# Two key-weight loads moved from SyncE's queue to ScalarE's at the start of a fused attention and GeGLU kernel

## The chip, the core and the metric

The kernel runs on one core of one Trainium2 chip. The time is the device time of that core in microseconds (us), from one launch to its end. Lower is better. Profiles are of one execution, taken by the hardware profiler.

## What is computed

The input x has 2048 rows of 640 values in bf16. The result mixes two blocks by a gate that each row computes for itself:

```python
g = sigmoid((x * gate_w).sum(-1))
qkv = x @ wqkv                      # 640 x 1920, 32 heads of 20
pq, pk = phi(q), phi(k)             # phi(t) = t + 1 where t > 0, else exp(t); plus 1e-6
kv = einsum("bhsd,bhse->bhde", pk, v); z = pk summed over the rows
a = (pq @ kv) / (pq . z + 1e-6) @ wo
b = (gelu(x @ w_gate) * (x @ w_up)) @ w_down     # 640 x 1728, 1728 x 640
out = g * a + (1 - g) * b
```

## The kernel before

The rows are taken in 16 tiles of 128. Every matmul contracts over 128 partitions, so the 640 input features make five chunks, numbered 0 to 4, and a product of a row tile with a 640-wide weight is five steps. A step needs the transposed tile (features on the partitions, `xT`) as the stationary operand and one chunk of 128 weight rows as the moving one.

All instructions are recorded in program order by a small planner (`P.op`), one list for each engine. It works out from the buffers read and written which semaphores an instruction waits for; it reorders nothing. So the order in the source is the order on each engine, and the order of the DMAs on each of the two queues that issue them, SyncE's (SP) and ScalarE's (ACT).

The order of work on TensorE (PE) is:

1. The first stage, which the change is in. A few matmuls on constants (`warm`), then the transposes of row tile 0 on TensorE (`T`, L439, copied out by VectorE in L443), then the key products of row tiles 0 to 3, and then their query products. `KM(n, [k])` is one step, chunk k, of the key product of row tile n: one matmul over 512 columns (L459) and one over 128 (L460), into two PSUM banks of the tile's own. `QM` (L474, L475) is the same for queries, with one extra column, the gate. `gate_col` (L504, L506) turns the gate weights into that column. After each of these products `phi1` (ScalarE, L484 and L488) and `phi2` (VectorE, L494 and L498) apply phi.
2. Key and query products of row tiles 4 to 15 (`KQ`, L545).
3. The sums over rows (`MM`, L602, L605, L612, L617), the feed-forward's first two products (`G`, L706), the small attention matrices (`KV`, `W2`), and the output products (L827 to L880).

The first stage's inputs come from DRAM. `load_x` (L349) brings a row tile as it is; `load_wk` (L352) brings one chunk of the key weights, 128 rows of 1280 bytes, 160 KB; `load_wq` (L360) one chunk of the query weights; all three end in `dma_in`, whose one line the profile calls L343. `load_xT` (L355) is a transposing DMA that writes row tile i straight into `xT`. Row tile 0 alone is transposed by TensorE. `gw_sb` holds the gate weights. The loads are put into the two queues like this (the first of ScalarE's is a load of 128 bytes, L368):

```python
load_x(0)
load_wk(0)
load_xT(1)
load_wk(3)
load_wk(4)
load_wk(1, "act")
load_wk(2, "act")
# then on ScalarE: the Exp table's load (L379), gate weights (L381)
for i in range(2, NQ): load_xT(i)      # NQ = 4
for k in range(KC): load_wq(k)         # KC = 5
for i in range(NQ, NT): load_xT(i)     # NT = 16
```

Behind these, SyncE issues the other big loads (the rest of x, the gate, up, value and output weights). In this text x0 is the plain load of row tile 0, xT1 to xT15 are the transposing loads, wk0 to wk4 the key chunks, wq0 to wq4 the query chunks.

TensorE takes the key products of row tiles 0 and 1 in this order: KM(0) with chunks 0, 1, 2; KM(1) with chunks 0, 1, 2; KM(0) with 3; KM(1) with 3; `gate_col`; KM(0) with 4; KM(1) with 4. Row tiles 2 and 3 follow, each with all five chunks in a row.

Of the kernel before, what the change touches and what calls it, by code (L numbers as in the profile page):

```python
# [16 lines left out]
KC = D // 128  # L17
# [145 lines left out]
def bass_gated_mix__linear_attn_block__geglu_ffn__prompt_kernel(  # L163
# [63 lines left out]
    with (  # L227
# [8 lines left out]
        with contextlib.ExitStack() as stack:  # L236
# [105 lines left out]
            def dma_in(dst, src, writes, reads=(), eng="sp"):  # L342
                P.op(eng, lambda e, dst=dst, src=src: e.dma_start(dst, src),  # L343
                     reads=reads, writes=writes, dma=new_dma_key())
# [6 lines left out]
            def load_wk(k, eng="sp", after=()):  # L351
                dma_in(wk[:, k, :], A_wqkv[k * 128:(k + 1) * 128, 640:1280], [r_wk[k]], reads=after, eng=eng)  # L352

            def load_xT(i, after=()):
                P.op("sp", lambda e: e.dma_start_transpose(xT[:, :, i * 128:(i + 1) * 128],  # L355
                                                           A_x[0, i * 128:(i + 1) * 128, :]),
                     reads=list(after), writes=[r_xT[i]], dma=new_dma_key())
# [12 lines left out]
            load_x(0)  # L370
            load_wk(0)
            load_xT(1)
            load_wk(3)
            load_wk(4)
            load_wk(1, "act")
            load_wk(2, "act")

            zero = nc.const_aps.tensor(0.0, (128, 1), F32)
            P.op("act", lambda e: e.activation(eg[:, 0:1], zero, ACT.Exp), writes=[r_eg[0]])  # L379
# [41 lines left out]
            def warm(count, n):  # L421
                def fn(e):
                    last = None
                    for w in range(count):
                        last = e.matmul(ps[:, 4, 0:n], one_l, one_r[:, 0:n], start=True, stop=True)
                    return last
                P.op("pe", fn, writes=[bank[4]])
# [4 lines left out]
            def slot(n):  # L432
                return SLOTS[n % 4]
# [17 lines left out]
            def KM(n, ks):  # L451
                i = seq[n][1]
                b0, b1 = slot(n)

                def fn(e):
                    last = None
                    for k in ks:
                        lhs = xT[:, k, i * 128:(i + 1) * 128]
                        e.matmul(ps[:, b0, :], lhs, wk[:, k, 0:512], start=(k == 0), stop=(k == KC - 1))  # L459
                        last = e.matmul(ps[:, b1, 0:128], lhs, wk[:, k, 512:640],  # L460
                                        start=(k == 0), stop=(k == KC - 1))
                    return last
                P.op("pe", fn, reads=[r_xTa[i] if i < NXN and ks == [0] else r_xT[i]] + [r_wk[k] for k in ks],
                     writes=[bank[b0], bank[b1]])
# [37 lines left out]
            def gate_col():  # L502

                P.op("pe", lambda e: e.matmul(ps[:, 7, 0:5], gw_sb, ident[:, 0:5], start=True, stop=True),  # L504
                     reads=[r_gw, r_ident], writes=[bank[7]])
                P.op("dve", lambda e: e.tensor_copy(wq[:, :, 640:641], ps[:, 7, 0:5].unsqueeze(2)),  # L506
                     reads=[bank[7]], writes=[r_gcol])
# [4 lines left out]
            T(0, [0], 7)  # L512
            T(0, [1, 2, 3, 4], 6)
            warm(2, 128)
            for k in range(3):
                KM(0, [k])
            for k in range(3):
                KM(1, [k])
            KM(0, [3])
            KM(1, [3])  # L520
            gate_col()
            KM(0, [4])
            KM(1, [4])
            ALLK = list(range(KC))
            for n in range(2 * NQ):
# [419 lines left out]
```

## Time and profile before

| | |
|---|---|
| time, median of 3 runs | 273.60 us (273.55 to 273.61) |
| the profiled execution's own time | 273.49 us |
| its span, first to last instruction | 272.2 us |
| TensorE matmul busy | 267.0 us, 98% of the span |
| VectorE, ScalarE, GpSimd busy | 140.9, 76.0, 30.6 us |
| granted TensorE clock | 1.00 |

The profiled execution took 1.3 us longer than its span, and 0.1 us less than the median of the runs. Times inside the span are counted from its start. PE is TensorE's matmuls, PEld its weight loads, DVE VectorE; SPq and ACTq are the queues of SyncE and ScalarE, where an entry is the issuing of a DMA and not its transfer. In the lists of DMA queues, q1 carries what SyncE issues and q10 what ScalarE issues; a packet is one row of 1280 bytes of a plain load, one piece of 256 bytes of a transposing one, or a 4-byte mark.

### The profile page before, as it was taken

Reading aid. Unit: us, or ns where it says so; the run is one execution under the profiler, and the core shown is the slowest. Engines: PE = TensorE matmul, PEld = TensorE weight load, DVE = VectorE, ACT = ScalarE, POOL = GpSimd, SP = SyncE. Lnnn points to the kernel's source line nnn. Section 1 sums busy time; section 2 is a strip of 40 time slices with the busy share of each in tenths; the row PEclk is TensorE's granted clock in tenths of the full one; section 3 lists DMA queues with packets and bytes.
Section 4 is the critical chain, followed back from the end, with each engine's and each line's share of the span. In section 5 each row is a group of like instructions: output and inputs, shape, how many; then the busy total and the mean of one; then the engine's idle time right before and its main releaser. Section 6 shows DMA issues by size and latency. Waiting matters only on the chain.

```text
span 272.2 us, 3462 instructions
## 1 busy us (share of the span) xinstructions
PE 267.0 (98%) x1366; PEld 127.2 (47%) x1392; DVE 140.9 (52%) x248; ACT 76.0 (28%) x132; POOL 30.6 (11%) x30
## 2 busy tenths in 40 slices
PE   7999999999999999999999999999999999999997
PEld 3555555544445454444444444444444444444444
DVE  1678989997234335999999999634110000000200
ACT  2455555210422453332222232224011122121021
POOL 6000000003240002242332421000000000000000
DMA  7976999610200011614121221262031110110221
GB/s 192 203 117 120 356 401 379 117 3 19 58 19 2 23 52 48 198 28 52 24 48 29 46 48 25 60 233 94 2 78 40 39 39 19 41 39 19 58 60 39
DMA packets 42680, 23.61 MB, mean 87 GB/s; under 512 B 32167, under 2 KB 41255, under 8 KB 42535
## 3 DMA queue, kind: packets, MB, share of 16 engines
q1 hardware_dynamic: 42333, 23.05, 32.2%
q10 hardware_dynamic: 330, 0.33, 0.4%
q8 instruction: 11, 0.18, 0.3%
q14 instruction: 6, 0.05, 0.1%
HBM read 13.67 MB, written 2.63 MB: 60 GB/s over the span
## 4 chain that ended last, share of the span: by engine, by line
PE 96%; DMA 1%; SPq 1%; issue 1%; DVE 0%
PE ps L706 41%; PE ps L880 23%; PE ps L545 12%; PE ps L602 6%; PE ps L859 4%; PE ps L684 2%; PE ps L474 2%; PE ps L827 2%; PE ps L605 1%; DMA pool<-in_A_x_dram 1%; PE ps L459 1%; PE ps L840 1%; SPq L343 1%; SPq L355 0%; PE ps L755 0%
## 5 line engine op out<-in xcount | busy, mean ns | idle before, releaser
L706 PE MATMUL ps<-pool 128*128 128x512 bf16 x509 | 112.8, 379 | 0.7 <-issue 0.2
L706 PEld LDWEIGHTS ps<-pool 128*128 128x128 bf16 x520 | 50.6, 98 | 60.3
L880 PE MATMUL ps<-pool 128*128 128x512 bf16 (+2 forms) x300 | 62.2, 366 | 0.5 <-issue 0.2
L712 ACT ACTIVATE pool<-ps 128x512 f32<-128x512 f32 x52 | 31.1, 597 | 72.8 <-PE ps L706 70.1
L714 DVE TENSOR_TENSOR pool<-ps,pool 128x512 bf16<-128x512 f32 x52 | 34.7, 688 | 31.1 <-PE ps L706 29.8
L880 PEld LDWEIGHTS ps<-pool 128*128 128x128 bf16 x306 | 29.2, 98 | 33.4 <-issue 0.4
L863 DVE TENSOR_TENSOR pool<-ps,pool 128x512 bf16<-128x512 f32 x4 | 2.8, 692 | 61.5 <-PE ps L859 59.4
L545 PE MATMUL ps<-pool 128*128 128x512 bf16 (+1 forms) x176 | 32.5, 343 | 0.2
L770 POOL TENSOR_TENSOR pool<-pool 128x640 f32<-128x640 bf16 x16 | 22.5, 1406 | 72.6 <-DVE pool L772 65.8
L887 ACT ACTIVATE pool<-ps,pool 128x512 bf16<-128x512 f32 (+1 forms) x16 | 10.9, 681 | 68.6 <-PE ps L880 68.6
L545 PEld LDWEIGHTS ps<-pool 128*128 128x128 bf16 x180 | 17.6, 98 | 15.0
L564 DVE SCALAR_TENSOR_TENSOR pool<-ps,pool 128x128 bf16<-128x128 f32 (+2 forms) x36 | 21.7, 603 | 2.1
L555 ACT ACTIVATE pool<-ps 128x640 bf16<-128x640 f32 x24 | 16.9, 704 | 15.8 <-DVE pool L564 9.3
L602 PE MATMUL ps<-pool 128*128 128x512 bf16 x76 | 19.2, 379 | 0.1
L780 DVE TENSOR_TENSOR pool<-pool 128x640 bf16<-128x640 bf16 x16 | 13.2, 825 | 0.6
L778 DVE TENSOR_SCALAR pool<-pool 128x32 f32<-128x32 f32 x16 | 12.8, 802 | 0.6
L772 DVE TENSOR_REDUCE pool<-pool 128x32 f32<-128x640 f32 x16 | 12.9, 807 | 0.0
L650 DVE TENSOR_TENSOR pool<-pool 128x640 f32<-128x640 f32 x14 | 11.6, 825 | 0.5
L859 PE MATMUL ps<-pool 128*128 128x512 bf16 x51 | 11.4, 379 | 0.0
L652 POOL PARTITION_ALL_REDUCE pool<-pool x1 | 4.0, 3972 | 60.2 <-DVE pool L650 60.2
L602 PEld LDWEIGHTS ps<-pool 128*128 128x128 bf16 x78 | 6.9, 98 | 7.3
L561 DVE TENSOR_SCALAR pool<-pool 128x640 bf16<-128x640 bf16 x24 | 7.8, 326 | 1.7 <-ACT pool L555 0.4
(73 smaller groups left out, 123.4 us busy)
## 6 DMA issues: line engine op xcount, KB each, us to landing
out_dram<-pool SPq DMA_DIRECT2D x19, 128.0 KB, 1.7
pool<-in_B_w_gate_dram SPq DMA_DIRECT2D x1, 2080.0 KB, 14.3
pool<-in_B_w_up_dram SPq DMA_DIRECT2D x1, 2080.0 KB, 18.4
pool<-in_A_wqkv_dram SPq DMA_DIRECT2D x8, 160.0 KB, 3.0
pool<-in_A_x_dram SPq DMA_DIRECT2D x1, 1280.0 KB, 9.3
pool<-in_A_x_dram SPq DMA_DIRECT2D x1, 1120.0 KB, 6.4
pool<-in_B_w_down_dram SPq DMA_DIRECT2D x1, 1120.0 KB, 6.2
pool<-omg_row SPq DMA_DIRECT2D x1, 1024.0 KB, 4.8
```

Source lines behind the costliest of these rows:

```text
L545: last = e.matmul(ps[:, b + p, 0:c1 - c0], xT[:, k, i * 128:(i + 1) * 128], wkq[:, k, c0:c1], start=(k == 0), stop=(k == KC - 1))
L555: P.op("act", lambda e: e.activation(e_buf[m], ps_flat[:, o:o + 640], ACT.Exp), reads=banks, writes=[r_e[m]])
L564: P.op("dve", lambda e, c0=c0, c1=c1: e.scalar_tensor_tensor(dst[:, c0:c1], ps_flat[:, o + c0:o + c1], 1.0 + EPS, e_buf[m][:, c0:c1], ALU. ...
L602: last = e.matmul(ps[:, b, :], pk[i][:, c * 128:(c + 1) * 128], x_aug[:, i, 0:512], start=(i == 0), stop=(i == NT - 1))
L706: last = e.matmul(ps[:, b, :], w[:, k, fc * 128:(fc + 1) * 128], xT[:, k, j * 512:(j + 1) * 512], start=(k == 0), stop=(k == KC - 1))
L712: P.op("act", lambda e: e.activation(ge[n], ps[:, gb, :], ACT.Gelu_apprx_tanh), reads=[bank[gb]], writes=[r_ge[n]])
L714: P.op("dve", lambda e: e.tensor_tensor(hT[fc][:, j * 512:(j + 1) * 512], ps[:, ub, :], ge[n], ALU.mult), reads=[bank[ub], r_ge[n]], write ...
L770: P.op("pool", lambda e: e.tensor_tensor(tmp[n], pq[i], z_b, ALU.mult), reads=[r_pq[i], r_zb], writes=[r_tmp[n]])
L772: P.op("dve", lambda e: e.tensor_reduce(den[n], tmp[n].rearrange("p (h d) -> p h d", h=32), AX.X, ALU.add), reads=[r_tmp[n]], writes=[r_de ...
L780: P.op("dve", lambda e: e.tensor_tensor(pq[i].rearrange("p (h d) -> p h d", h=32), pq[i].rearrange("p (h d) -> p h d", h=32), den[n].unsqu ...
L859: last = e.matmul(ps[:, b, :], wd[:, fc, 512:640], hT[fc][:, j * 512:(j + 1) * 512], start=False, stop=(fc == NFC - 2), skip_group_check=True)
L880: last = e.matmul(ps[:, pb, 0:c1 - c0], lhs, rhs, start=False, stop=(q == len(rows) - 1), skip_group_check=True)
```

## The change

wk3 and wk4 are issued by ScalarE, behind wk1 and wk2, and no longer by SyncE between xT1 and xT2. SyncE's queue becomes x0, wk0, xT1, xT2, xT3, wq0 to wq4, xT4 and so on; ScalarE's becomes the 128-byte load, wk1, wk2, wk3, wk4, the Exp table, the gate weights. TensorE's order changes with it: row tile 0 takes its five chunks in a row, then row tile 1 its chunks 0 to 3, `gate_col`, and its chunk 4. No instruction is added or left out.

```diff
             load_x(0)
             load_wk(0)
             load_xT(1)
-            load_wk(3)
-            load_wk(4)
             load_wk(1, "act")
             load_wk(2, "act")
+            load_wk(3, "act")
+            load_wk(4, "act")
...
             warm(2, 128)
-            for k in range(3):
+            for k in range(KC):
                 KM(0, [k])
             for k in range(3):
                 KM(1, [k])
-            KM(0, [3])
             KM(1, [3])
             gate_col()
-            KM(0, [4])
             KM(1, [4])
```

## The prediction

> **What bounds the kernel now.** I read the page's busy line and its chain first, to see whether a shift at the start reaches the end.
>
> ```profile
> PE 267.0 (98%) x1366; PEld 127.2 (47%) x1392; DVE 140.9 (52%) x248; ACT 76.0 (28%) x132; POOL 30.6 (11%) x30
> PE 96%; DMA 1%; SPq 1%; issue 1%; DVE 0%
> ```
>
> TensorE is the bound, nearly without a gap. The waits of PE over the whole span (engine, line and what it waited for; total, times, longest) are these:
>
> ```profile
> PE ps L425 <- PEq L930: 0.8, 1, 0.8
> PE ps L459 <- DMA pool<-in_A_wqkv_dram: 0.5, 1, 0.5
> PE ps L459 <- DMA pool<-in_A_x_dram: 0.4, 1, 0.4
> ```
>
> Apart from the launch, the longest waits are both at L459, the key products of the first stage. So whatever moves the end of those products moves the end of the kernel by as much: behind them the chain is matmuls to the last tile, with pieces of 0.05 us of "issue" and no wait of 0.3 us that could swallow a delay or give more back. Next the chain's start (start, length, what):
>
> ```profile
> 1.71 1.31 SPq L355
> 3.01 0.05 issue
> 3.06 0.57 SPq L343
> 3.64 0.04 issue
> 3.68 0.43 SPq L343
> 4.11 0.04 issue
> 4.15 3.90 DMA pool<-in_A_x_dram
> 8.05 0.05 issue
> 8.10 0.39 PE ps L459
> ```
>
> xT1's issue, wk3's, wk4's, then xT2 from issue to landing, then KM(2). This is what the change attacks: it takes the two L343 pieces out. The timeline of PE around it shows where TensorE stands:
>
> ```profile
> 4.45 0.43 PE L459 MATMUL ps<-pool 128*128 128x512 bf16 x1 [0.48 <-DMA pool<-in_A_wqkv_dram]
> ...
> 5.26 0.22 PE L460 MATMUL ps<-pool 128*128 128x128 bf16 x1
> 5.90 0.39 PE L459 MATMUL ps<-pool 128*128 128x512 bf16 x1 [0.42 <-DMA pool<-in_A_x_dram]
> ...
> 7.78 0.22 PE L460 MATMUL ps<-pool 128*128 128x128 bf16 x1
> 8.10 0.39 PE L459 MATMUL ps<-pool 128*128 128x512 bf16 x1
> ```
>
> A step of KM starts every 0.27 us (5.90, 6.18, 6.45, 6.72, 6.99), and the gate column adds 0.03 (7.27, next step 7.29). Chunks 0 to 2 of tile 0 could have been followed at 5.31; KM(1) began at 5.90, when xT1 had landed (issued 1.71, 4.1 to landing, so 5.85). That is 0.59 lost. KM(1)'s last step ended its turn at 7.83; KM(2) began at 8.10, held by xT2: 0.27 lost. Together 0.86 us, 0.3% of the time, is all that the stage can give. About 0.2% (0.55 us) is what a measurement of this kernel tells from no change.
>
> Last, the DMA queues, since the change only pays if transfers land earlier. Queue lines of three stretches: 3.75 to 4.4, 5.15 to 5.9 and 5.9 to 6.9 (packets, MB, share of the 16 engines).
>
> ```profile
> q10 hardware_dynamic: 148, 0.15, 66.0%
> q1 hardware_dynamic: 208, 0.06, 43.8%
> ...
> q1 hardware_dynamic: 193, 0.23, 101.1%
> ...
> q1 hardware_dynamic: 716, 0.20, 96.2%
> ```
>
> The engines are full from 3 us on, and where both queues have work they divide it: while wk2 runs on q10, xT1 on q1 gets 208 small packets and only 0.06 MB. The second stretch is plain rows alone: 0.23 MB in 0.75 us, so a key chunk (0.164 MB) takes about 0.5 us of all engines. The third holds xT2's 640 pieces: about 0.95 us for a transposing load.
>
> **The change, part by part.**
>
> SyncE: two issues go, 0.57 and 0.43 with their gaps, 1.09 us. xT2 is issued at 3.06 instead of 4.15, xT3 at about 4.35, wq0 at 5.63 instead of 6.72, all later DMAs of SyncE 1.09 earlier. The later ones are worth nothing: wq0 landed at about 9.3 (6.72 plus 2.6) and its first reader ran at 10.82; xT4 landed at 13.3 and was read at 16.27.
>
> ScalarE: two issues of 0.46 (the pair of wk1 and wk2 took 0.93), so wk3 is issued at 2.16, wk4 at 2.62. The Exp table moves from 2.20 to about 3.1, and with 1.28 + 0.20 us is done by 4.7; ScalarE idled until 7.76, and its first phi now comes at 6.3 at the earliest. That cover is 1.6 us. The gate weights are issued at about 3.15 instead of 2.27, behind two more chunks on q10. I bound their landing by wk4's plus the time of a short load: 6 to 7 us against a reader at 7.7 or later: nothing. On VectorE the gate column's copy stands ahead of phi of tile 0, which is now ready earlier and waits there; the query product that needs those banks runs at about 11, against 9.7 when phi of tile 0 ended before. Nothing.
>
> TensorE: the same matmuls in another order. Tile 0 wants wk3 and wk4 at once. With issue to landing as for wk1 and wk2 (3.3 each) they land at 5.5 and 5.9; KM(0) then ends at about 6.25, and if xT1 is there, KM(1) takes five steps and the gate, 1.39 us.
>
> xT1 is the open cost. wk3 and wk4 used to run behind it on q1; now they run on q10 right behind wk2, which ended at about 4.4, and xT1's pieces (3.8 to 5.1 in the trace) are under way just then. Bounds: none (xT1 keeps 5.85), or both chunks ahead of xT1's end, 2 x 0.5 = 1.0 us. Nearest row: the first stretch above, where q10 held its own against q1. If the queues take turns packet by packet, 256 rows pass while 256 of xT1's some 450 last pieces do; both chunks are through before it ends, and nearly the whole 1.0 is paid. I take 0.9: xT1 at about 6.75.
>
> The Trainium skill's page "DMA: Bandwidth & Descriptors", section "Queues, rings and completion order", says that each DMA engine goes round-robin between the queues at packet granularity, and "Issuing engines are not separate DMA queues" says that a second issuing engine saves only issue time. The stretch agrees (148 packets against 208). By the rule xT1 pays the 1.0 us and the result is 273.9; if the queues were independent it would be 273.1.
>
> A second open cost is how a transposing load completes. By the packet counts xT2's pieces were through at 6.9, yet it landed at 8.05, 1.15 later; it was followed by another transposing load. xT1 and xT3 were followed by plain loads; their pieces ended at 5.1 and 8.3, and they landed at 5.85 and 8.8, 0.75 and 0.5 later. The change puts xT2 directly behind xT1. Bounds: 0 and 0.4 us (1.15 less 0.75). I take 0.1 to 0.2, for the cause is only guessed.
>
> Sum: xT1 at 6.75 + 0.15 = 6.9; KM(1) from 6.95, KM(2) at 8.34 instead of 8.10. xT2's pieces follow xT1's, from about 6.0 to 7.0, and even 1.15 later it lands at 8.15: just in time. xT3 lands at about 8.7 and is read at 9.7. Change: +0.25 us. On the profiled 273.49 that is 273.74; the median of the runs stands 0.1 higher: about 273.9. By the bounds of both costs the forecast's own range is 273.5 to 274.15. The wait moves from xT2 to xT1; two short waits become one long one.
>
> **Rivals.**
>
> 1. xT1 isn't delayed (5.85). wk4 lets KM(0) end at 6.25, KM(1) at 7.63, and xT2, at 3.06 + 3.9 to 4.1, is there at 7.2. KM(2) starts 0.47 earlier: 273.1, just inside the bound of 0.2%; only if wk4 too came sooner would it pass it. For it: xT1 is issued before wk3 and had begun before wk2 ended. Against it: the full engines.
> 2. Slower. Consecutive transposing loads stall the engines before xT1 completes. In this stretch between xT2 and xT3, from 7.6 to 7.9, hardly anything moved:
>
> ```profile
> q1 hardware_dynamic: 41, 0.01, 66.3%
> ```
>
> 0.3 us with 41 packets, where others carry 190 or more. If that falls between xT1 and xT2, 0.3 to 0.45 comes on top of the forecast's 6.9: xT1 at 7.2 to 7.4, or more with the full 0.4 of late completion. KM(2) starts at 8.65 to 9.0: 274.2 to 274.6. It decides as soon as xT1 lands after 7.2.
> 3. TensorE's clock falls back. Its first matmuls of 512 columns ran at 0.43 us each, later ones at 0.22. With one wait of some 0.6 instead of 0.59 and 0.27 apart I hold that unlikely; five steps at half speed would cost 1.4 us: 275.
> 4. The change doesn't do what it says: xT2 no longer gates, but wk4 on ScalarE's full queue comes as late as before (6.8) and KM(1) follows it: 7.1 + 1.39 = 8.5, +0.4: 274.0.
>
> **How the numbers follow.** Forecast 0.50, rival 1 0.14 (0.05 of it past the bound), rival 2 0.27, rival 3 0.05, rival 4 0.04. Faster 0.05; slower 0.27 + 0.05 = 0.32; same 0.63. The predicted time is the forecast's, 273.9. The range runs from rival 1's better half, 273.2, to rival 2's upper end, 274.6.
>
> **What would show it.** Right: KM(0)'s five steps nearly together, ending at about 6.2 to 6.4; one wait at L459 for a load of x that ends near 6.9; KM(2) without a wait; more q10 packets between 4.2 and 5.6, and q1's pieces of xT1 lasting to about 6. Wrong: xT1 landing at 5.9 (rival 1); after 7.2, or a stretch with few packets before it (rival 2); a later wait on PE that takes a shift back; L459 spaced wider than 0.27 after a wait (rival 3).

## The result: 1% slower, and the profile after

| | before | after |
|---|---|---|
| median of 7 runs | 273.48 us (273.14 to 273.61) | 276.30 us (274.43 to 278.13) |
| ratio | | 1.0099 (1.0073 to 1.0125) |
| the profiled execution's own time | 273.49 us | 276.44 us |
| its span | 272.2 us | 275.2 us |
| KM(2) starts | 8.10 us | 11.03 us |

The changed kernel is slower by 2.8 us in the median, outside the range given, and its executions spread over 3.7 us where those of before, measured beside them, lie within half a microsecond. The page's busy line and chain of the profile after:

```profile
PE 268.3 (97%) x1366; PEld 127.7 (46%) x1392; DVE 141.0 (51%) x248; ACT 76.0 (28%) x132; POOL 30.5 (11%) x30
PE 96%; DMA 2%; issue 1%; ACTq 0%; DVE 0%
```

TensorE is still the bound. The longest waits of PE (engine, line and what it waited for; total, times, longest):

```profile
PE ps L459 <- DMA pool<-in_A_wqkv_dram: 2.6, 3, 1.5
PE ps L425 <- PEq L928: 0.8, 1, 0.8
PE ps L704 <- issue: 0.2, 1, 0.2
```

The waits at L459 went from 0.9 to 2.6 us, and none is put down to x any more: all three are for key chunks. The start of the chain (start, length, what):

```profile
1.71 0.46 ACTq L343
2.20 5.42 DMA pool<-in_A_wqkv_dram
7.67 0.61 PE ps L459
```

wk3, issued by ScalarE at 2.20, took 5.42 us to land, where wk1 and wk2 on the same queue had taken 3.3 in the kernel before. The timeline of PE shows what came of it:

```profile
5.69 0.39 PE L459 MATMUL ps<-pool 128*128 128x512 bf16 x1 [0.47 <-DMA pool<-in_A_wqkv_dram]
5.91 0.22 PE L460 MATMUL ps<-pool 128*128 128x128 bf16 x1
7.67 0.61 PE L459 MATMUL ps<-pool 128*128 128x512 bf16 x1 [1.53 <-DMA pool<-in_A_wqkv_dram]
...
8.76 0.63 PE L459 MATMUL ps<-pool 128*128 128x512 bf16 x1
...
9.29 0.63 PE L459 MATMUL ps<-pool 128*128 128x512 bf16 x1
...
11.03 0.38 PE L459 MATMUL ps<-pool 128*128 128x512 bf16 x1
```

A wait of 1.5 us for wk3 (7.67), and behind it steps every 0.53 us instead of 0.27. The windows name the reason (stretch, length, busy time of PE, PEld, DVE, ACT, POOL; then the granted clock, the DMA share and GB/s):

```profile
4.00:5.00 1.00, 0.48 (x3) 0.28 (x4) 0.26 (x1) 0.65 (x2) 0.81 (x4) 1.00 1.12 221
5.00:6.00 1.00, 0.53 (x4) 0.11 (x2) 0.00 (x0) 0.00 (x0) 0.42 (x1) 1.00 1.24 128
6.00:7.00 1.00, 0.13 (x2) 0.00 (x0) 0.00 (x0) 0.00 (x0) 0.00 (x0) 1.00 1.05 160
7.00:7.50 0.50, 0.00 (x0) 0.00 (x0) 0.00 (x0) 0.00 (x0) 0.00 (x0) 0.64 1.48 274
7.50:10.00 2.50, 2.33 (x9) 1.04 (x10) 0.00 (x0) 0.70 (x1) 0.00 (x0) 0.50 1.13 289
10.00:10.40 0.40, 0.40 (x4) 0.14 (x2) 0.00 (x0) 0.00 (x0) 0.00 (x0) 0.50 1.06 355
10.40:11.00 0.60, 0.60 (x7) 0.32 (x6) 0.03 (x1) 0.00 (x0) 0.00 (x0) 0.87 1.07 369
```

The granted clock fell to half during the wait, between 7.0 and 7.5, and came back after 10.4. At full clock, wk4 (landed 8.2) and xT1 (8.35) would have let KM(1) start at 8.5 and KM(2) at 9.9. So of the 2.93 us by which KM(2) is late in this execution, 1.8 are transfers and 1.1 the clock. The whole difference is there: 2.93 us at KM(2), 2.95 us in the execution's time.

Where the transfers went shows in the queue lines of one and the same stretch, 4.75 to 6.25, of the kernel before and then of the changed one (packets, MB, GB/s; then each queue's packets, MB, share of the 16 engines):

```profile
DMA packets 737, 0.43 MB, mean 290 GB/s; under 512 B 481, under 2 KB 737, under 8 KB 737
q1 hardware_dynamic: 735, 0.43, 110.7%
```
```profile
DMA packets 360, 0.18 MB, mean 123 GB/s; under 512 B 268, under 2 KB 360, under 8 KB 360
q10 hardware_dynamic: 98, 0.12, 74.0%
q1 hardware_dynamic: 262, 0.07, 40.1%
```

With xT1 on q1 and wk3 on q10 the engines move 123 GB/s instead of 290. They don't divide a fixed rate; the rate itself falls to less than half.

### The profile page after: what moved, and what is told of

It reads as the page before. It is cut to its first block, busy times and chain, and to the rows that moved or that the text cites. A ratio compares the mean times of both kernels' runs of the same rounds, so it can differ in the third digit from the quotient of the medians.

```text
span 275.2 us, 3462 instructions
## 1 busy us (share of the span) xinstructions
PE 268.3 (97%) x1366; PEld 127.7 (46%) x1392; DVE 141.0 (51%) x248; ACT 76.0 (28%) x132; POOL 30.5 (11%) x30
## 4 chain that ended last, share of the span: by engine, by line
PE 96%; DMA 2%; issue 1%; ACTq 0%; DVE 0%
PE ps L704 41%; PE ps L878 23%; PE ps L543 12%; PE ps L600 6%; PE ps L857 4%; DMA pool<-in_A_wqkv_dram 2%; PE ps L459 2%; PE ps L682 2%; PE ps L474 2%; PE ps L825 2%; PE ps L603 1%; PE ps L838 1%; PE ps L460 0%; PE ps L753 0%; PE ps L475 0%
## 5 line engine op out<-in xcount | busy, mean ns | idle before, releaser
L704 PE MATMUL ps<-pool 128*128 128x512 bf16 x509 | 112.8, 379 | 0.7 <-issue 0.2
L553 ACT ACTIVATE pool<-ps 128x640 bf16<-128x640 f32 x24 | 16.9, 703 | 15.8 <-DVE pool L562 9.3
L600 PE MATMUL ps<-pool 128*128 128x512 bf16 x76 | 19.2, 379 | 0.1
L857 PE MATMUL ps<-pool 128*128 128x512 bf16 x51 | 11.4, 379 | 0.0
L459 PE MATMUL ps<-pool 128*128 128x512 bf16 x19 | 7.1, 449 | 2.6 <-DMA pool<-in_A_wqkv_dram 2.6
```

What stands on the lines that cost most here:

```text
L553: P.op("act", lambda e: e.activation(e_buf[m], ps_flat[:, o:o + 640], ACT.Exp), reads=banks, writes=[r_e[m]])
L600: last = e.matmul(ps[:, b, :], pk[i][:, c * 128:(c + 1) * 128], x_aug[:, i, 0:512], start=(i == 0), stop=(i == NT - 1))
L704: last = e.matmul(ps[:, b, :], w[:, k, fc * 128:(fc + 1) * 128], xT[:, k, j * 512:(j + 1) * 512], start=(k == 0), stop=(k == KC - 1))
L857: last = e.matmul(ps[:, b, :], wd[:, fc, 512:640], hT[fc][:, j * 512:(j + 1) * 512], start=False, stop=(fc == NFC - 2), skip_group_check=True)
```

## The experiments

**1. The changed kernel again.** The kernel is unaltered; this gives a second profile and more times.

> The changed kernel once more, unaltered, for a second profile and more times. Theory M (mixing): a transposing load on SyncE's queue and plain rows on ScalarE's, in flight together, slow each other far beyond taking turns (the first profile: 0.44 MB from 4.4 to 7.2 us, 159 GB/s, against 244 to 302 GB/s in nearby stretches of before). It expects again wk3, wk4 and xT1 to land between 6.5 and 8.5, and 274.4 to 278 us, depending on how the turns fall and whether TensorE's clock falls back. Rival R (row): the transposing loads issued back to back hold up one another's completion, whatever ScalarE's queue does: xT1 late, but wk3 at 5.5 to 6. Rival C (clock): the transfers cost little, and nearly all of the loss is the clock at half: then an execution without a fallback takes about 273.9.

Measured: median 276.11 us (274.65 to 277.65), ratio 1.0112 (1.0081 to 1.0143). The profiled execution took 274.65 us. wk3 landed at 7.0, xT1 at 7.2, wk4 at 7.5, and 4.75 to 6.25 moved 140 GB/s:

```profile
DMA packets 349, 0.21 MB, mean 140 GB/s; under 512 B 228, under 2 KB 349, under 8 KB 349
q10 hardware_dynamic: 125, 0.15, 95.7%
q1 hardware_dynamic: 224, 0.06, 21.6%
```

In this one the steps ran 0.48 and 0.54 apart until 5.5, and at full clock from there on, and KM(2) started at 9.23: 1.13 later than before, for an execution 1.16 us longer. So the transfers alone cost over 1.1 us; rival C, which gave them next to nothing, falls.

**2. The queues alone.** The loads as changed, TensorE's order as before:

```diff
-            for k in range(KC):
+            for k in range(3):
                 KM(0, [k])
             for k in range(3):
                 KM(1, [k])
+            KM(0, [3])
             KM(1, [3])
             gate_col()
+            KM(0, [4])
             KM(1, [4])
```

> Half of the change: the loads of wk3 and wk4 on ScalarE's queue, TensorE's order as before (tile 0 chunks 0-2, tile 1 chunks 0-2, then 3 and 4). Theory M: the transfers are as late as in the changed kernel (xT1 near 8, wk3 near 7.6), TensorE waits once, for xT1 from 5.3 on; KM(2) starts at 10.3 or, with the clock down, 11: 275.5 to 277 us. Rival O (order): the loss comes from tile 0 now needing wk3 and wk4 at once; with the old order it is back at 273.5 or better. Rival R: xT1 late by up to 1.4, wk3 on time: 274.2 to 274.6.

Measured: median 276.12 us (274.49 to 278.11), ratio 1.0095 (1.0057 to 1.0133). The longest wait of PE in its profile is now for xT1:

```profile
PE ps L459 <- DMA pool<-in_A_x_dram: 1.5, 1, 1.5
```

KM(2) starts at 9.34, earlier than the 10.3 of theory M, as the transfers are about a half microsecond less late than it took them to be (xT1 7.35, wk3 7.1), and that execution took 274.78 us. The queues alone make the whole loss.

**3. TensorE's order alone.** The other half: the kernel before with the new order of steps.

> The other half: TensorE's order as in the changed kernel, the loads' queues as before. Theory M: wk3 lands at 6.25, wk4 at 6.8 as before; KM(0) ends at 7.1, KM(1) at 8.5, KM(2) starts 0.4 us later than before: 273.8 to 274.0 us, clock full throughout. Rival O: 275 us or more, like the changed kernel.

Measured: median 273.82 us, ratio 1.0009 (0.9993 to 1.0025); in the profile KM(2) starts at 8.56, 0.46 later than before, and the execution took 273.96 us, 0.47 more. As expected from the sum: wk3 and wk4, now needed at once, land at 6.2 and 6.8 as before. 4.75 to 6.25 moved 272 GB/s. Rival O falls.

**4. TensorE kept busy in the changed kernel.**

```diff
             for k in range(KC):
                 KM(0, [k])
+                if k == 2:
+                    warm(8, 512)
```

> The changed kernel with 8 matmuls on constants (512 columns, 0.22 us each at full clock, 1.7 us) after tile 0's chunk 2, into the bank that the warm-up uses: TensorE is kept busy while it waits for wk3. Theory M with a clock part: the transfers land as in the changed kernel, no step is spaced 0.53, KM(2) starts at about 9.9 instead of 11.0: 275.0 to 275.5 us, and the times of the rounds lie closer together. Rival C: the whole loss goes: 273.5 to 274. Without any part of the clock: 276.3 and more, as the filler then only costs.

Measured: 274.73 us, all four executions between 274.61 and 274.76; ratio 1.0042 (1.0027 to 1.0057). The waits of PE in its profile:

```profile
PE ps L425 <- PEq L930: 0.8, 1, 0.8
PE ps L459 <- DMA pool<-in_A_wqkv_dram: 0.2, 1, 0.2
```

The transfers are as late as ever (wk3 7.2, xT1 7.8, wk4 7.6; 188 GB/s from 4.5 to 5.5 and 146 from 5.5 to 6.5), and KM(2) starts at 9.35, earlier than expected (9.9, for 275.0 us and more). But TensorE has no long gap in which to lose its clock, no step runs at half speed, and the spread of these four is 0.15 us instead of 3.7. Eight useless matmuls win 1.4 to 1.6 us. So the loss has two layers: 1.2 us of late transfers, and up to 3.4 us more that depends on the execution and goes when TensorE is kept busy. That the clock makes the second layer is shown for the profile after (0.50 from 7.5 to 10.4); for the longest executions, whose granted clock is 1.00, it is inferred.

**5. The transposing loads in a row, but no key chunk beside them.**

```diff
-            load_xT(1)
-            load_wk(1, "act")
-            load_wk(2, "act")
-            load_wk(3, "act")
-            load_wk(4, "act")
+            load_wk(3)
+            load_wk(4)
+            load_xT(1)
+            load_wk(1, "act")
+            load_wk(2, "act")
```

> The transposing loads xT1, xT2, xT3 in a row as in the changed kernel, but wk3 and wk4 on SyncE's queue ahead of them (x0, wk0, wk3, wk4, xT1, xT2, xT3), so that only wk1 and wk2 are on ScalarE's and all key chunks are through before xT1's pieces begin; TensorE's order as changed. Theory M (mixing): xT1's pieces run alone from about 4.9 to 5.9, it lands at 6.3 to 7.0; KM(2) starts at 7.8 to 8.4: 273.2 to 273.9 us, no fallback of the clock. Rival R (row): in a row they hold each other up: xT1 at 7.2 or later, KM(2) at 8.6 or later: 274.0 us and more.

Measured: median 274.16 us (273.31 to 275.89), ratio 1.0020 (0.9997 to 1.0042). Neither theory as written. xT1 landed at 7.35, as the rival R has it, but what TensorE waited for was a plain load, wk2, until 6.5, which R doesn't touch. The four plain loads ahead did not end together: a few rows on each queue, at most three in 0.25 us, were still running from 5.5 to 6.2 when xT1's pieces had begun, and the stretch from 5.25 to 6.5 again moved 123 GB/s. From 5.63 to 6.16 these last rows come from the two queues in turn, one every 52 ns: the pattern of a single engine, for whose backlog the pieces of the others seem to wait. That gave the idea for experiments 9 and 10.

**6. The transposing loads not in a row.** The changed kernel with wq0 and wq1 between xT1 and xT2:

```diff
+            load_wq(0)
+            load_wq(1)
             for i in range(2, NQ):
                 load_xT(i)
-            for k in range(KC):
+            for k in range(2, KC):
                 load_wq(k)
```

> The changed kernel with wq0 and wq1 between xT1 and xT2 on SyncE's queue: wk3 and wk4 still on ScalarE's and still beside xT1, but the transposing loads not in a row behind it. Theory M: wk3 and xT1 still slow each other, though only for xT1's own 640 pieces: both at 6.3 to 7.2, wk4 at 7 to 7.5, xT2 later than 8.5: 274.0 to 274.8 us, or more where the clock falls back. Rival R: xT1 at about 6, wk3 at 5.5: the time is set by xT2, about 274.0, with KM(1) done by 7.6.

Measured: median 275.42 us (274.38 to 278.10), ratio 1.0072 (1.0045 to 1.0099). wk3 lands at 7.0, xT1 at 7.2, wk4 at 7.7; 150 GB/s from 4.75 to 6. KM(2) starts at 9.40, later than in the changed kernel's own second profile. Rival R falls as the cause: without other transposing loads right behind xT1 most of the loss stays.

**7. Mixing by itself, later.** The kernel before, with the load of row tiles 1 to 7 issued by ScalarE behind the first stage:

```diff
-            dma_in(x_aug[:, NXN:8, 0:640], ..., r_xn[NXN:8])
...
                 phi1(n)
                 phi2(n)
+            dma_in(x_aug[:, NXN:8, 0:640], ..., r_xn[NXN:8], eng="act")
```

> The kernel before, with one load moved: the plain load of row tiles 1 to 7 (1.12 MB; SyncE issued it at 25.5 us behind the last transposing load, and it landed 6.4 us later, alone) is issued by ScalarE behind the phi of the first stage, about 17 us, beside xT8 to xT15. It measures the mixing by itself, where TensorE has nothing to wait for. Theory M: rows take 120 to 270 ns each instead of 55 to 65, the load takes 10 us or more, the transposing loads of that stretch land later than their 3.2 to 4.4 us, and while both run the engines move less than 200 GB/s. Rival S (plain sharing): the engines, busy three quarters of that stretch, take it up at 250 GB/s and more, row times stay near 60 to 90 ns. Time either way 273.3 to 273.8, as xT8 and on are read from 30 us.

Measured: 273.69 us, ratio 0.9998 (0.9983 to 1.0013); the load landed 6.5 us after its issue, not 10 or more. Theory M is missed in this and in the rate, and right only in that transposing loads land later. The queue lines from 20.5 to 22.25, where both run steadily, and from 17.5 to 18.75, where rows begin:

```profile
DMA packets 828, 0.64 MB, mean 364 GB/s; under 512 B 413, under 2 KB 828, under 8 KB 828
q10 hardware_dynamic: 415, 0.53, 83.1%
q1 hardware_dynamic: 413, 0.11, 26.6%
```
```profile
DMA packets 196, 0.09 MB, mean 75 GB/s; under 512 B 146, under 2 KB 196, under 8 KB 196
q10 hardware_dynamic: 50, 0.06, 49.2%
q1 hardware_dynamic: 146, 0.03, 12.7%
```

In the steady stretch rows and pieces go one for one (415 and 413) at 364 GB/s. So standing beside each other is not by itself what costs the engines' rate; the transposing load only gets one packet for each row, and its issue to landing rose to 7.8 us for the one issued at 15.8. The beginning is slower, 75 GB/s where the kernel before moved 126 in the same stretch. Stalls without any row on ScalarE's queue also exist: in the kernel before, 16.6 to 17.15 moved 39 packets at 18 GB/s, soon after a single packet of instructions, 16 KB, that held one engine for 1.05 us from 15.36 on. Whether that packet is the cause was not tested.

**8. Row tile 1 transposed by TensorE.** The kernel before with `NXN = 2` and:

```diff
-            load_xT(1)
+            load_x(1)
...
             for k in range(3):
                 KM(0, [k])
-            for k in range(3):
-                KM(1, [k])
+            T(1, [0], 7)
+            T(1, [1, 2, 3, 4], 6)
             KM(0, [3])
-            KM(1, [3])
-            gate_col()
             KM(0, [4])
+            for k in range(4):
+                KM(1, [k])
+            gate_col()
             KM(1, [4])
```

> A version without transposing loads among the key chunks: row tile 1 comes by a plain load in xT1's place on SyncE's queue and is transposed by TensorE like row tile 0 (5 small matmuls, 2 copies on VectorE) after tile 0's chunk 2; then tile 0's chunks 3 and 4, then tile 1. wk1, wk2 stay on ScalarE's queue, wk3, wk4 on SyncE's. Theory M: the plain loads run unmixed, wk3 and wk4 land by 5.2 to 5.8, xT2's pieces run alone from about 5.2 and it lands by 7.0 to 7.3; KM(2) starts at about 7.4 instead of 8.1: 272.7 to 273.1 us. If transposing loads cost the same wherever they stand, and only the number in front counts, the gain is the half microsecond by which a plain load is shorter: 273.0 to 273.2.

Measured: median 274.97 us (273.48 to 275.71), ratio 1.0034 (1.0011 to 1.0057). A miss. Plain rows on both queues share the engines without loss (326 GB/s from 3 to 5 us), but then wk0 is held up by its share, to 4.85, and TensorE idles 1.0 us at the moment its clock should be coming up: in the profile its steps run at 0.53 until 9.7. Its best execution is level with before, so I found no version that beats both.

**9 and 10. One slow DMA engine, and none.** The kernel before with one extra load of n rows, n = 31 and n = 32, beside the transposing loads at 17 us:

```diff
                 phi1(n)
                 phi2(n)
+            dma_in(m_sb[0:31, 0, :], A_wqkv[0:31, 0:640], [r_m[0]], eng="act")
```

> The kernel before, with one small extra load: 31 rows of 1280 bytes (40 KB) issued by ScalarE behind the phi of the first stage, about 17 us, into a buffer not yet in use, beside the transposing loads xT8 and xT9. If the 31 rows come one behind another (31 x 55 ns = 1.7 us) they sit on one DMA engine. Theory H (lockstep: a transposing load advances at the pace of its slowest engine, and its held-back pieces hold up the other engines): for 1.5 to 2 us the pieces of all engines fall from 100-190 per 0.25 us to under 30, and the transposing load of that moment lands 1 us or more late. Rival S (plain sharing): only that engine's share, 1/16, is late; the other pieces flow on. Time 273.3 to 273.8 either way.

> The same with 32 rows instead of 31. If the rows spread over the engines they take some 0.1 us together. Theory H: no stall of the pieces, so that the stall of the kernel with 31 rows comes from the one slow engine and not from the bytes or from ScalarE's queue. If it stalls like the other, theory H falls: then a transposing load beside any rows of the other queue is slow. Time 273.3 to 273.8.

Measured: 273.79 us (273.40 to 274.43), ratio 1.0015 (1.0005 to 1.0026), and 273.85 us (273.64 to 274.50), ratio 1.0013 (1.0003 to 1.0023): both are 0.2 to 0.3 us longer. In the profiles 0.17 and 0.24 us of that stand already at KM(2), long before the extra load is issued at 16.7, so how much of it the load costs is open. The queue lines from 19 to 20.4, with 31 rows and then with 32:

```profile
DMA packets 29, 0.03 MB, mean 20 GB/s; under 512 B 9, under 2 KB 29, under 8 KB 29
q1 hardware_dynamic: 9, 0.00, 23.1%
q10 hardware_dynamic: 20, 0.03, 4.9%
```
```profile
DMA packets 965, 0.23 MB, mean 167 GB/s; under 512 B 965, under 2 KB 965, under 8 KB 965
q1 hardware_dynamic: 965, 0.23, 85.1%
```

The clearest result of the study. The last 22 of the 31 rows follow one another from 19.38 to 20.5, one every 52 ns, as on one engine: q10's share is 4.9% of sixteen engines, less than one. The 32 spread, and are through in 0.5 us, by 18.4. In the 1.4 us in which the last of the 31 rows run, all the transposing loads together move 9 pieces; in the same stretch of the other kernel, with its rows gone, 965. While the 32 rows passed (17.5 to 18.5) 449 packets of the transposing loads moved in 1 us. From issue to landing the transposing load issued at 14.4 took 6.3 us and 4.8. So in this stretch one engine with a backlog stops the pieces of all sixteen: a transposing load advances with its slowest engine. Theory H holds here.

The Trainium skill's page "DMA: Bandwidth & Descriptors", section "Why a DMA increments its semaphore by 16 and not by 1", says how rows are spread: the largest number of engines up to 16 that divides the row count. 31 and 32 rows agree with it. That a transposing load stands still for one late engine I take from these two runs alone.

**11. A smaller dose.** The kernel before, with wk4 alone moved to ScalarE's queue, TensorE's order as before:

```diff
             load_wk(3)
-            load_wk(4)
             load_wk(1, "act")
             load_wk(2, "act")
+            load_wk(4, "act")
```

> A smaller dose: wk4 alone on ScalarE's queue (behind wk1 and wk2), wk3 stays between xT1 and xT2 on SyncE's; TensorE's order as before. 128 rows instead of 256 stand beside xT1's last pieces. Theory H: the stall comes as soon as rows are left at the end of xT1's pieces, so xT1 lands at 6.4 to 7.1, most of what the whole change costs; 274.0 to 275.5 us. Rival S: xT1 pays 0.5 us (6.35), xT2 is issued 0.47 earlier, KM(2) starts at 8.0 to 8.3: 273.4 to 273.8.

Measured: median 274.80 us (274.05 to 277.58), ratio 1.0068 (1.0042 to 1.0094). xT1 lands at 6.9, 1.1 later than before, and TensorE waits 1.1 us for it. KM(2) starts at 8.91, 0.8 later, and 4.75 to 6.25 moved 225 GB/s. With half the rows that is two thirds of the loss by the ratio and by KM(2), under half by the medians (1.2 of 2.8 us). xT1's landing lies in theory H's range and not at rival S's 6.35, but whether the price goes with the number of rows or falls due as soon as some are left, one dose doesn't decide.

**12. Fillers in the kernel before.**

```diff
             warm(2, 128)
+            warm(1, 512)
             for k in range(3):
                 KM(0, [k])
+            warm(2, 512)
```

> The kernel before with three matmuls on constants more (512 columns): one ahead of tile 0's chunk 0, two ahead of tile 1's chunk 0, in the two gaps where TensorE waits for wk0 and xT1. The clock theory: the kernel before also falls back in some executions (5 of 50 beside these runs took 274.7 to 275.4); with the gaps filled these are gone, all times lie within 273.2 to 274.0, and the median stays at 273.5. If the outliers have another cause they stay, one in ten.

Measured: 273.62 us (273.40 to 274.13), ratio 1.0006 (0.9997 to 1.0015). No time above 274.3 in 11, but the kernel before beside it had none in 32 either. Beside experiments 1 to 8 it had six in 50, of 274.7 to 275.4 us; what makes these stays undecided.

## Why the prediction was wrong

**What held.** The reading that this stage alone decides, and that each shift of KM(2) reaches the end in full, held within 0.05 us in all these profiles but one:

| profile | KM(2) later than before | execution longer by |
|---|---|---|
| changed kernel | 2.93 us | 2.95 us |
| again (1) | 1.13 | 1.16 |
| queues alone (2) | 1.24 | 1.29 |
| order alone (3) | 0.46 | 0.47 |
| TensorE kept busy (4) | 1.25 | 1.25 |
| row ahead (5) | 0.69 | 0.73 |
| not in a row (6) | 1.30 | 1.33 |
| tile 1 by TensorE (8) | 2.20 | 2.21 |
| wk4 alone (11) | 0.81 | 0.98 |

In the last one 0.14 us came on top near 50 us, ahead of L602; its reason is not known.

SyncE's issues moved up by 1.0 us, nearly as worked out (wq0 at 5.70), and the Exp table was done by 4.7. The landing of the gate weights is not in the profile, but the last packet on ScalarE's queue ran at 7.5, 3.2 us before their reader.

**The step that failed** is the price of xT1's meeting with wk3 and wk4, "Bounds: none ..., or both chunks ahead of xT1's end, 2 x 0.5 = 1.0 us". It took for granted that full engines stay at one rate and only divide it. xT1 landed at 8.35 and 7.2 in the two profiles, 2.5 and 1.4 later than before, where at most 1.0 was allowed for the meeting (1.4 with the second open cost). The runs show a stall in its place. From 4.75 to 6.25 the engines moved 123 GB/s in the changed kernel, 140, 161, 148 and 177 in the others with both chunks on ScalarE's queue at xT1's end (experiments 1, 2, 4, 6), and 225 with one chunk (11), but 290 and 272 in the two kernels that have them behind xT1 on SyncE's queue (before and experiment 3). Taking turns packet by packet, drawn from the row of 148 and 208 packets, was right as far as it goes (415 and 413 in experiment 7); what a turn costs was not.

**The same error decided the time through another term:** "With issue to landing as for wk1 and wk2 (3.3 each) they land at 5.5 and 5.9". The meeting was priced for xT1 alone, not for the rows. wk3 took 5.4 and wk4 5.5 us, and they landed at 7.6 and 8.2; in experiment 1 at 7.0 and 7.5. In both profiles of the changed kernel TensorE waits at L459 for these key chunks, inside or at the end of tile 0's five steps, and not for xT1, as the forecast had it. The new order of steps matters little for that: with the old one TensorE waits as long for xT1 (experiment 2).

The lower end of the forecast's own range, 273.5, does not follow from its bounds: with no cost for xT1 the sum is rival 1's 273.1. The upper end nearly does (274.2), and the measured time lies far beyond it.

**The clock**, rival 3, was given 0.05, "With one wait of some 0.6". The wait is 1.5 us, and in the first profile the clock did fall, at a cost of 1.1 us against the rival's 1.4. Its chance hung on the step before it. The length of the wait doesn't decide alone: in experiment 2's profile one of 1.5 us was followed by steps at 0.27.

**Rival 2** had the right sign and named a stall before xT1 completes, but put it down to consecutive transposing loads. Experiment 6 takes the row apart and the stall stays. The 0.3 us between 7.6 and 7.9 of the profile before, by which it was priced, is a stall too, though with no row of ScalarE's queue in flight; whether it has the same cause isn't shown. But this row could have told that the engines' rate is not a constant.

**What stays open.** Experiments 9 and 10 show the lockstep at 17 us, not at 5 us. The last rows of experiment 5 look like the same thing at 6 us. For the changed kernel itself it is not shown, and its queue lines speak against a single late engine: from 4.75 to 6.25 the rows on q10 took 74% of all sixteen engines' time, and in experiment 1 96%, where the 31 rows took 4.9%. A row took some 180 ns there on average, instead of 55 (worked out from these shares and the 98 and 125 packets). Why rows and pieces slow each other so is open. So are the two longest executions of the changed kernel, 277.3 and 278.1 us, in which the granted clock shows no drop; in experiment 8 the steps ran at half speed until 9.7 with a granted clock of 1.00, so a late warm-up may hide there, but neither of the two has a trace here.

## What to carry to other kernels

Moving a load to a second queue doesn't only change when it is issued but whom it meets: of the orders tried here, the one with the plain loads behind the transposing load on the same queue was the best, and loads ahead of it cost as soon as some of their rows were unfinished (experiment 5). When engines are full, look for stretches where they move half their usual rate before assuming that a change merely divides it. And a wait at the start of a kernel can cost more than its idle time: one of 1.5 us cost another 1.1 us through TensorE's clock in one execution and nothing in another, and a few matmuls on constants in the gap took that part away.

## What the runs showed of the hardware

- TensorE's clock fell to half though its longest idle time was 1.5 us: in the profile after, PE was busy 1.14 us of the 3 us from 4 to 7, then the granted clock was 0.50 for some 3.4 us (an estimate from the rows with 0.64 and 0.87 at its two ends: about 7.1 to 10.55). The Trainium skill's page "TensorE: Matmul & The Clock Gate", section "What's actually happening", has it fall after an idle window of about 3.4 us, a window that runs by itself and doesn't start with the kernel. A free-running window would explain why the same wait cost some executions nothing; but no fully idle window was needed here. The phase differs between executions: the steps of tile 0 ran at 0.27 from 4.5 on in the profile after, whose clock then fell, and 0.48 to 0.54 apart until 5.5 in that of experiment 1, whose clock then stayed.
- In experiments 9 and 10 a transposing load advanced with its slowest DMA engine: with 31 rows following one another all engines moved 9 pieces in 1.4 us, where without rows they moved 965.
- In a steady state a row of 1280 bytes and a piece of 256 take turns one for one, at 364 GB/s together.
